# Normalising the transposed attention output from SBUF, and moving the dV products, in a one-core backward kernel

## The chip, the core and the metric

The kernel runs on one core of a Trainium2 chip. A core has a matrix engine (TensorE, PE in the profile), a vector engine (VectorE, DVE), an activation engine (ScalarE, ACT), a general engine (GpSimd, POOL) and a queue engine (SyncE, SP), each of which works through its own list of instructions in order and waits on semaphores for the others. Matrix products land in PSUM, which here is cut into eight banks of 128 partitions x 512 fp32; everything else lies in SBUF or in device memory. PEld in the profile is the loading of a matrix product's stationary operand.

The metric is the device time of one execution in microseconds (us). Before the change, three executions took 1052.82, 1053.05 and 1053.12 us, median 1053.05.

## What is computed

Two attention blocks over 2048 tokens of width 448 with 16 heads of 28, side by side, and the gradients of all their inputs and weights for a given `grad_out`. Block A is a linear attention; it fills the first 200 us and the change does not touch it. Block B is a multi-query attention, one key and one value head shared by 16 query heads:

```
scores = einsum("bhqd,bkd->bhqk", q, k) * (Dh ** -0.5)
p = _softmax(scores, axis=-1)
o = einsum("bhqk,bkd->bhqd", p, v)
out = o (heads side by side) @ wo
```

and `jax.vjp` of it: with dO the gradient of o, the kernel needs dV = P^T dO, dP = dO V^T, dS = P * (dP - D) with D the row sum of dO * o, dQ = dS K and dK = dS^T Q. The change lies in block B's main loop.

## The kernel before, in words

**Blocks and units.** The loop `for u in range(NU + 28)` (L926) runs over NU = 512 units. Eight units make a block b (64 blocks): a block is two heads (a pair) and 256 queries; a unit is 256 of the 2048 keys, in two halves of 128. "Unit 2 of a block" below is u = 8b + 2, and so on. Scores are kept transposed, keys on partitions. The work of one block is spread over several blocks' time: in the pass u the loop does the scores and exponentials of unit u, and the dP and dS of unit w = u - 16.

**One pass.** PE, in `rows_SD` (L683), writes the scores of two heads into two banks `sp` (S0, S1) of a ring of three, `SB`, and dP of unit w into the two banks `DB` (D0, D1); each bank takes two matmuls, one for each half of the keys, and uses 32 of the PE's rows: S0 and S1 lie on one half of the rows, D0 and D1 on the other. `todo` is the order of the eight matmuls. ACT then does exp of S0 (L946), a copy of D1 to SBUF, `cp` (L960), and exp of S1 (L992). DVE multiplies D0 by the exponentials of unit w (L958), POOL multiplies `cp` by those of the other head (L961); both write `dsT`. DVE transposes, in 32x32 blocks, the `dsT` of two passes earlier (L1039, `dsx`). There is only one D0 and one D1 bank: PE can write D0 of the next pass only after L958 has read this one, and D1 after L960.

**What PE does behind the rows.** Odd units: `dk_m`, sixteen matmuls for dK. Even units: `o_dq`, sixteen matmuls for o and dQ of two earlier units; the o sums of a block end in unit 0 of the next one. Behind `o_dq`, three of the four even units add dV: `dv_mm` multiplies one quarter (one head and 128 queries: four matmuls over 512 columns) of a block's dO/l, `don`, with the transposed exponentials `eN`. Two quarters come in unit 4, one in unit 6, one in unit 2 (L1006-1008).

**Once a block.** These steps borrow the third bank of `SB` for one pass, `spare` (L932). It was the S1 bank of the pass before, so it is free when that pass's L992 has read it, and it becomes the S0 bank of the next pass, whose first matmul therefore waits until the borrower has been read:

- unit 0: one part of the output projection (`out_proj`, sixteen small matmuls; in the early blocks `do_proj`), read by DVE at L747 (L913);
- unit 1: DVE copies o out of its bank to `oTs` (L974);
- unit 2: PE transposes `oTs` into the spare bank (`onat_T`, L809), and `o_norm` (L813) divides: DVE takes the reciprocal of the sums l out of the bank (L818, four elements a partition) and multiplies the bank by it into `oTs` (L819, 128 elements). POOL then forms `prod` = dO * o (L823), `don` = dO / l (L826), and copies o (L827);
- unit 3: DVE moves dQ out of its bank (L977); unit 4: DVE sums `prod` (L831), POOL scales the sum into `don` (L832);
- unit 6: PE transposes `don` into the spare bank (`don_T`, L840), DVE copies it (L847).

POOL further issues the store of a finished output tile once in four blocks (L749) and copies pieces of q (L851), up to two a block, in half of the blocks.

**What sets the order.** `tc.manual_schedule()`: each engine's instructions stand in the order in which the loop issues them, with no planner. So on DVE a pass is L958, then the once-a-block steps, then L1039. On PE a pass is the rows, then the once-a-block transposes or projection, then `dk_m` or `o_dq` with dV.

Of the kernel before, what the change touches and what calls it, by code (L numbers as in the profile page):

```python
# [9 lines left out]
ALU = mybir.AluOpType  # L10
# [7 lines left out]
P = 128  # L18
# [7 lines left out]
def kernel(  # L26
# [21 lines left out]
    nc = tc.nc  # L48
# [598 lines left out]
    NB = 64  # L647
# [3 lines left out]
    with ExitStack() as cs_:  # L651
# [20 lines left out]
        def eN(b, c):  # L672
            return ENs[(2 * b + c // 2) % 6][:, 16 * (c % 2):16 * (c % 2) + 16, :]

        def mmt(out, lhsT, rhs, pos, start, stop):
            nc.tensor.matmul(out, lhsT=lhsT, rhs=rhs, start=start, stop=stop, tile_position=pos,  # L676
                             skip_group_check=True)

        def blk(b):
            qc, pair = divmod(b, 8)  # L680
            return qc, pair, pair // 2, pair % 2

        def rows_SD(u, sp, dp):  # L683
            b, tp = divmod(u, 8)
            w = u - 16
            qc, pair, g, hp = blk(b)
            todo = [(0, 0), (0, 1), (1, 0), (1, 1)] * 2
            if sp is not None and dp is not None and u % 2 == 0:
                todo = [(0, 0), (0, 1), (1, 0)] * 2 + [(1, 1)] * 2
            seen = {}  # L690
            for d in todo:
                if (dp if d[0] else sp) is None:
                    continue
                k, h = d
                t2 = seen.get(d, 0)
                seen[d] = 1
                t = 2 * tp + t2
                tc_ = slice(t * P, (t + 1) * P)
                oc = slice(t2 * 256, (t2 + 1) * 256)
                r = 64 * (1 - hp if k else hp) + 32 * h  # L700
                if k:
                    mmt(dp[h][:, oc], vT_rep[r:r + 32, tc_], doT[w // 8][r:r + 32, :], (r, 0), True, True)
                else:
                    mmt(sp[h][:, oc], kT_rep[r:r + 32, tc_], qT_B[g][r:r + 32, qc * 256:(qc + 1) * 256],
                        (r, 0), True, True)
# [96 lines left out]
        def due(u, lag):  # L802
            b, r = divmod(u - lag, 8)
            return b if r == 0 and 0 <= b < NB else None

        def onat_T(b, bank):
            onp = bank[:, 0:P].rearrange("p (q h c) -> p q h c", q=2, h=2)
            for qb in range(2):
                nc.tensor.transpose(onp[:, qb, :, :].rearrange("p h c -> p (h c)"), oTs[0:64, qb * P:(qb + 1) * P],  # L809
                                    identF[0:64, 0:64], tile_position=(0, 0))  # L810
            onps[b] = onp

        def o_norm(b):  # L813
            onp = onps.pop(b)
            qc, pair, g, hp = blk(b)
            r_ = pw_.tile([P, 2, 2, 1], F32, name="rl")
            os_ = oTs[:, 0:P].rearrange("p (q h c) -> p q h c", q=2, h=2)
            nc.vector.reciprocal(out=r_[:], in_=onp[:, :, :, 0:1])  # L818
            nc.vector.tensor_tensor(out=os_, in0=onp[:, :, :, :], in1=r_[:].to_broadcast([P, 2, 2, 32]), op=ALU.mult)  # L819
            rl[b] = r_  # L820
            dnv = do_nat[:, 2 * qc:2 * qc + 2, pair * 64:pair * 64 + 64].rearrange("p q (h c) -> p q h c", c=32)
            prod[b] = pw_.tile([P, 2, 2, 32], F32, name="prod", bufs=1)
            nc.gpsimd.tensor_tensor(out=prod[b][:], in0=dnv, in1=os_, op=ALU.mult)  # L823
            dn = pw_.tile([P, 2, 2, 32], BF16, name="don", bufs=3)
            don[b] = dn
            nc.gpsimd.tensor_tensor(out=dn[:], in0=dnv, in1=r_[:].to_broadcast([P, 2, 2, 32]), op=ALU.mult)  # L826
            nc.gpsimd.tensor_copy(out=dnv, in_=os_)  # L827
# [32 lines left out]
        def dk_m(b, m, other=0):  # L860
            qc, pair, g, hp = blk(b)
            h, B, s = m // 8, (m // 2) % 4, m % 2
            for a in range(4):
                rhs = dsx[b][32 * a:32 * a + 32, :, h, :, :].rearrange(
                    "p u t (b i s) -> p u t b i s", b=4, s=2)[:, :, :, B, :, s]
                k = 32 * ((a + 2) % 4) if other else 32 * a
                mmt((dk_two if other else dk_acc)[k:k + 32, :],
                    qX[qc][32 * a:32 * a + 32, B, s, pair * 64 + 32 * h:pair * 64 + 32 * h + 32],
                    rhs, (32 * a, k), other == 2 or b == 0 and m == 0, other == 0 and b == NB - 1 and m == 15)
# [19 lines left out]
        def o_dq(vs, ys):  # L889
            for v, y in zip(vs, ys):  # L890
                todo = [f(i) for f, i in ((o_mm, v), (dq_mm, y)) if 0 <= i < NU]
                for _ in range(2):
                    for g_ in todo:
                        next(g_)

        def dv_mm(dv_acc, b, h, qb):
            for c in range(4):
                rhs = eN(b, c).rearrange("p (u h t q) k -> p u h t q k", u=2, h=2,
                                                       t=2)[:, :, h, :, qb, :]
                mmt(dv_acc[32 * c:32 * c + 32, :], don[b][:, qb, h, :], rhs, (0, 32 * c),  # L900
                    b == 0 and h + qb == 0, b == NB - 1 and h + qb == 2)
# [15 lines left out]
        with tc.manual_schedule():  # L917
# [8 lines left out]
            for u in range(NU + 28):  # L926
# [3 lines left out]
                sp = [SB[(2 * u + h) % 3] for h in range(2)] if hasS else None  # L930
                dp = DB if hasD else None
                spare = SB[(2 * u + 2) % 3] if hasS else DB[u // 4 % 2] if u > 530 else SB[2]  # L932
                rows_SD(u, sp, dp)
                if (b := due(u, 10)) is not None:
                    onat_T(b, spare)
                if (b := due(u, 14)) is not None:
# [10 lines left out]
                if u == 1:  # L947
                    q_shift(pn3, shifts[3], [pd_.tile([P, 2, 512], BF16, name="dsT").rearrange("p a b -> p (a b)").bitcast(F32)
                                             for _ in range(1)])
                    dv_acc = psA.tile([P, 512], F32, name="aacc")  # L950
# [24 lines left out]
                if (b := due(u, 27)) is not None:  # L975
                    qc, pair, g, hp = blk(b)
                    nc.vector.tensor_scalar(out=qT_B[g][64 * hp:64 * hp + 64, qc * 256:(qc + 1) * 256],  # L977
                                            in0=oq[64:128, 0:256], scalar1=scale, scalar2=None, op0=ALU.mult)
                if (b := due(u, 10)) is not None:
                    o_norm(b)  # L980
                    if b in (15, 31, 47, 55, 63):
                        t0, t1 = 2 * (b // 8) - 2 * (b < 48), 2 * (b // 8) + 2
                        nc.sync.dma_start_transpose(oTq[:, 4 * (t0 % 4):4 * (t0 % 4) + 4 * (t1 - t0), :],
                                                    do_nat[:, t0:t1, :].rearrange("p q c -> p (q c)"))
# [14 lines left out]
                if u % 2:  # L999
                    b, i = divmod(u - 27, 8)  # L1000
                    if 0 <= b < NB:
                        for m in range(2 * i, 2 * i + 4):
                            dk_m(b, m, (1 + (u == 519 and m == 2 * i + 1)) * (m % 2) if 519 <= u < 537 else 0)
                else:
                    o_dq((u - 2, u - 1), (u - 20, u - 19))
                    b, n = divmod(u - 20, 8)  # L1006
                    for k in {0: (0, 1), 2: (2,), 6: (3,)}.get(n, ()) if 0 <= b < NB else ():
                        dv_mm(dv_acc, b, k // 2, k % 2)
                y = u - 18

                if 512 <= u < 528 and u % 2 == 0:
# [23 lines left out]
                if 0 <= y < NU:  # L1035
                    b, tp = divmod(y, 8)
                    if tp == 0:
                        dsx[b] = px_.tile([P, 8, 2, 2, 256], BF16, name="dsx")
                    nc.vector.transpose(  # L1039
                        out=dsx[b][:, tp, :, :, :].rearrange("p h t c -> p (h t c)").bitcast(F32),  # L1040
                        in_=dsT[y][:, :, :].rearrange("p h c -> p (h c)").bitcast(F32))
# [14 lines left out]
        for c in range(4):  # L1056
# [3 lines left out]
                                           in1=dk_sum[32 * c:32 * c + 32, :].rearrange("p (t i) -> p t i", i=32),  # L1060
# [91 lines left out]
```

## Time and profile before

| | |
|---|---|
| three executions | 1052.82, 1053.05, 1053.12 us |
| profiled execution | 1052.68 us, span on the core 1050.9 us, granted clock 1.00 |
| busy over the span | PE 96%, DVE 85%, ACT 83%, POOL 76% |
| block A and block B's projections | up to about 207 us; first exp of the loop at 207.7 us |
| two blocks in the middle | 495.20 to 507.23 us (12.03 us) and 507.23 to 519.20 us (11.97 us) |
| DVE in those two | busy 11.82 and 11.77 us |
| ACT in those two | busy 11.96 and 11.90 us |
| POOL in those two | busy 10.37 and 10.85 us |

Busy times on the page are unions of spans, and spans of neighbours on one engine overlap by some 80 ns where they follow each other at once: a span holds the end of the pipeline, in which the next instruction already starts. So what an instruction takes from its engine is the distance from its start to the start of the next one, called its step here, and an engine that is never idle is recognised by steps that are always the same. Once the loop is full, its blocks take alternately 12.03 and 11.97 us, with few exceptions: odd blocks and even blocks differ by the half of the partitions on which their heads lie.

### The profile page before, as it was taken

How to read it: one execution, taken by the hardware profiler on the slowest of the kernel's cores; microseconds unless marked ns; L12 is line 12 of the kernel's file. 1: busy time of each engine (PE TensorE's matmuls, PEld its weight loads, DVE VectorE, ACT ScalarE, POOL GpSimd, SP SyncE). 2: the span in 40 equal slices, each digit the busy share in tenths (PEclk: the TensorE clock that was granted, in tenths of full speed). 3: DMA queues.
4: the chain of work that ended last, by engine and by line, in shares of the span. 5: the costliest groups of instructions: out<-in, count | busy, mean ns of one | idle time of the engine just before them, and what ended most of it. 6: DMA issues, size and time to landing. Idle time of an engine off the chain costs nothing.

```text
span 1050.9 us, 40033 instructions
## 1 busy us (share of the span) xinstructions
PE 1008.4 (96%) x16236; PEld 486.6 (46%) x16245; DVE 895.9 (85%) x1781; ACT 871.5 (83%) x1743; POOL 798.2 (76%) x1044
## 2 busy tenths in 40 slices
PE   9999999998999999999999999999999999999998
PEld 5555554434444444444444444444444444444444
DVE  6897500669999999999999999999999999999942
ACT  6463122589999999999999999999999999999632
POOL 8601272238888998899899989988998999888860
PEclk9999999999999999999999999999999999999999
DMA  9879999299999999999999999999999999999973
GB/s 266 150 134 192 189 222 215 42 163 202 188 196 190 188 195 198 194 193 191 197 175 195 192 202 185 204 199 184 192 194 191 194 190 193 204 186 182 220 156 87
DMA packets 689058, 195.15 MB, mean 186 GB/s; under 512 B 670408, under 2 KB 686688, under 8 KB 688872
## 3 DMA queue, kind: packets, MB, share of 16 engines
q1 hardware_dynamic: 680392, 179.97, 102.1%
q0 software_dynamic: 4544, 9.46, 3.4%
q10 hardware_dynamic: 3936, 3.16, 1.0%
q8 instruction: 127, 2.08, 0.8%
q14 instruction: 59, 0.48, 0.1%
HBM read 12.60 MB, written 10.84 MB: 22 GB/s over the span
## 4 chain that ended last, share of the span: by engine, by line
PE 44%; ACT 33%; issue 14%; DVE 6%; POOL 2%; DMA 0%; ACTq 0%; DVEq 0%; POOLq 0%
ACT cp L960 17%; ACT eT L992 13%; PE agen L81 13%; PE aacc L676 10%; PE agen L676 10%; PE aacc L81 6%; ACT eT L946 2%; DVE dsT L958 2%; PE aacc L809 2%; DVE dsx L1039 2%; PE aacc L840 1%; POOL dsT L961 1%; DMA out_dram<-dsT 0%; PE agen L313 0%; PE agen L227 0%
## 5 line engine op out<-in xcount | busy, mean ns | idle before, releaser
L961 POOL TENSOR_TENSOR dsT<-cp,eT 128x512 bf16<-128x512 bf16 x512 | 587.7, 1156 | 78.9 <-ACT cp L960 73.2
L1039 DVE STREAM_TRANSPOSE dsx<-dsT 128x512 f32<-128x512 f32 x512 | 357.8, 699 | 2.8 <-POOL dsT L961 0.7
L676 PEld LDWEIGHTS <-R 32*128 32x128 bf16 (+1 forms) x9104 | 228.5, 94 | 275.0 <-issue 239.4
L958 DVE TENSOR_TENSOR dsT<-agen,eT 128x512 bf16<-128x512 f32 x512 | 341.9, 668 | 10.6 <-PE agen L676 5.4
L960 ACT ACTIVATE cp<-agen 128x512 bf16<-128x512 f32 x512 | 315.8, 617 | 11.5 <-PE agen L676 10.5
L946 ACT ACTIVATE eT<-aacc 128x512 bf16<-128x512 f32 x512 | 313.6, 612 | 13.6 <-PE aacc L676 4.3
L992 ACT ACTIVATE eT<-aacc 128x512 bf16<-128x512 f32 x512 | 322.2, 629 | 0.0
L676 PE MATMUL agen<-dsx,qX 32*32 32x512 bf16 x4024 | 264.0, 376 | 0.0
L676 PE MATMUL agen<-doT,R 32*128 32x256 bf16 x2048 | 246.7, 269 | 4.2 <-DVE dsT L958 2.5
L676 PE MATMUL aacc<-R,R 32*128 32x256 bf16 (+1 forms) x2240 | 218.5, 269 | 7.1 <-DVE oTs L819 2.0
L676 PE MATMUL agen<-eT,R 128*32 128x256 bf16 x2048 | 157.4, 274 | 0.1
L676 PE MATMUL agen<-dsT,R 128*32 128x256 bf16 x2048 | 156.6, 274 | 0.1
L676 PEld LDWEIGHTS <-qX 32*32 32x32 bf16 x4096 | 78.2, 89 | 111.7 <-issue 53.3
L676 PE MATMUL aacc<-eN,don 128*32 128x512 bf16 x1024 | 96.7, 379 | 0.0
L81 PEld LDWEIGHTS <-R 128*128 128x128 bf16 x517 | 40.9, 98 | 42.2 <-issue 12.0
L81 PE MATMUL agen<-R,R 128*128 128x448 bf16 (+1 forms) x174 | 41.1, 360 | 1.8 <-ACT R L229 0.8
L851 POOL COPY qst<-R 128x512 bf16<-128x512 bf16 x56 | 34.2, 611 | 2.9 <-DMA qX<-qst 2.8
L823 POOL TENSOR_TENSOR prod<-R,oTs 128x128 f32<-128x128 bf16 x64 | 27.6, 431 | 9.3 <-DVE oTs L819 9.3
L676 PEld LDWEIGHTS <-don 128*32 128x32 bf16 x1024 | 33.8, 97 | 0.5
L586 DVE TENSOR_TENSOR osb<-R 32x512 bf16<-32x512 bf16 x4 | 1.7, 413 | 34.7 <-ACT R L583 34.7
L262 POOL TENSOR_SCALAR wdq<-wdq 128x448 bf16<-128x448 bf16 x16 | 21.1, 1327 | 12.9 <-DVE phiT L243 12.9
L427 POOL COPY pk<-R 128x256 bf16<-128x256 bf16 x4 | 1.6, 399 | 37.7 <-DVE R L389 37.7
(234 smaller groups left out, 983.1 us busy)
## 6 DMA issues: line engine op xcount, KB each, us to landing
eN<-eT SPq DMA_TRANSPOSE x128
xa<-in_A_x_dram SPq DMA_DIRECT2D x8, 224.0 KB
ga<-in_grad_out_dram SPq DMA_DIRECT2D x4, 448.0 KB
out_dram<-osb ACTq DMA_DIRECT2D x16, 112.0 KB
xa<-in_grad_out_dram POOLq DMA_DIRECT2D x4, 448.0 KB, 9.4
out_dram<-wdq POOLq DMA_DIRECT2D x8, 224.0 KB, 5.8
eT<-in_grad_out_dram SPq DMA_DIRECT2D x4, 448.0 KB
eT<-in_B_x_dram SPq DMA_DIRECT2D x4, 448.0 KB
```

The lines of the kernel that those rows point to most:

```text
L81: nc.tensor.matmul(out_ap, lhsT=lhsT, rhs=rhs, start=start, stop=stop, tile_position=(0, 0))
L262: nc.gpsimd.tensor_scalar(out=wq_n[:, st, 0:D], in0=wq_n[:, st, 0:D], scalar1=1.0, scalar2=None, op0=ALU.min)
L676: nc.tensor.matmul(out, lhsT=lhsT, rhs=rhs, start=start, stop=stop, tile_position=pos, skip_group_check=True)
L809: nc.tensor.transpose(onp[:, qb, :, :].rearrange("p h c -> p (h c)"), oTs[0:64, qb * P:(qb + 1) * P], identF[0:64, 0:64], tile_position=(0 ...
L823: nc.gpsimd.tensor_tensor(out=prod[b][:], in0=dnv, in1=os_, op=ALU.mult)
L851: eng.tensor_copy(out=st.rearrange("p (b s) a j -> p b s a j", s=2)[:, :, s, :, :], in_=src.unsqueeze(2).to_broadcast([P, 4, 4, 32]))
L946: nc.scalar.activation(out=eT(u)[:, 0, :], in_=sp[0][:, :], func=ACT.Exp, scale=scale)
L958: nc.vector.tensor_tensor(out=dst[:, 0, :], in0=dp[0][:, :], in1=ew[:, 0, :], op=ALU.mult)
L960: nc.scalar.activation(out=cp[:, :], in_=dp[1][:, :], func=ACT.Copy)
L961: nc.gpsimd.tensor_tensor(out=dst[:, 1, :], in0=cp[:, :], in1=ew[:, 1, :], op=ALU.mult)
L992: nc.scalar.activation(out=eT(u)[:, 1, :], in_=sp[1][:, :], func=ACT.Exp, scale=scale)
L1039: nc.vector.transpose(out=dsx[b][:, tp, :, :, :].rearrange("p h t c -> p (h t c)").bitcast(F32), in_=dsT[y][:, :, :].rearrange("p h c -> p ...
```

## The change

Three edits in the loop.

1. In `o_norm`, DVE first copies the transposed block (o and the sums l) out of the spare bank into `oTs`, then takes the reciprocal of the sums from `oTs`, then multiplies `oTs` by it in place. Before, the reciprocal and the product read the bank.
2. In `rows_SD`, odd units with both scores and dP take the order S0 S1 S0 S1 D0 D1 D0 D1 instead of S0 S1 D0 D1 S0 S1 D0 D1. Even units keep S0 S1 D0 S0 S1 D0 D1 D1 (the condition that kept the passes at either end of the loop out of this order is dropped).
3. The quarters of dV are issued right behind the rows instead of behind `o_dq`, and the quarter of unit 2 moves to unit 0 of the next block: two in unit 4, one in unit 6, one in unit 0.

```diff
-            todo = [(0, 0), (0, 1), (1, 0), (1, 1)] * 2
-            if sp is not None and dp is not None and u % 2 == 0:
+            todo = [(0, 0), (0, 1)] * 2 + [(1, 0), (1, 1)] * 2
+            if u % 2 == 0:
                 todo = [(0, 0), (0, 1), (1, 0)] * 2 + [(1, 1)] * 2
...
-            nc.vector.reciprocal(out=r_[:], in_=onp[:, :, :, 0:1])
-            nc.vector.tensor_tensor(out=os_, in0=onp[:, :, :, :], in1=r_[:].to_broadcast([P, 2, 2, 32]), op=ALU.mult)
+            nc.vector.tensor_copy(out=os_, in_=onp[:, :, :, :])
+            nc.vector.reciprocal(out=r_[:], in_=os_[:, :, :, 0:1])
+            nc.vector.tensor_tensor(out=os_, in0=os_, in1=r_[:].to_broadcast([P, 2, 2, 32]), op=ALU.mult)
...
                 rows_SD(u, sp, dp)
+                if u % 2 == 0:
+                    b, n = divmod(u - 20, 8)
+                    for k in {0: (0, 1), 2: (2,), 4: (3,)}.get(n, ()) if 0 <= b < NB else ():
+                        dv_mm(dv_acc, b, k // 2, k % 2)
...
                     o_dq((u - 2, u - 1), (u - 20, u - 19))
-                    b, n = divmod(u - 20, 8)
-                    for k in {0: (0, 1), 2: (2,), 6: (3,)}.get(n, ()) if 0 <= b < NB else ():
-                        dv_mm(dv_acc, b, k // 2, k % 2)
```

## The prediction, made before the changed kernel ran

> **What bounds the kernel now.** I read the page first, then busy times over two blocks of the loop, then DVE's timeline in them. On the page PE is the busiest engine and the loop looks full on four engines alike:
>
> ```profile
> PE 1008.4 (96%) x16236; PEld 486.6 (46%) x16245; DVE 895.9 (85%) x1781; ACT 871.5 (83%) x1743; POOL 798.2 (76%) x1044
> DVE  6897500669999999999999999999999999999942
> ACT  6463122589999999999999999999999999999632
> ```
>
> That does not say which one sets the pace, so I went to single steps. DVE's timeline over one odd block, 507.21 to 519.2:
>
> ```profile
> 507.92 0.28 DVE L747 CAST ot<-aacc 128x112 bf16<-128x112 f32 x1
> 508.11 0.70 DVE L1039 STREAM_TRANSPOSE dsx<-dsT 128x512 f32<-128x512 f32 x1
> 508.77 0.69 DVE L958 TENSOR_TENSOR dsT<-agen,eT 128x512 bf16<-128x512 f32 x1
> 509.38 0.41 DVE L974 COPY oTs<-agen 64x256 f32<-64x256 f32 x1
> ...
> 510.33 0.64 DVE L958 TENSOR_TENSOR dsT<-agen,eT 128x512 bf16<-128x512 f32 x1
> 510.91 0.16 DVE L818 RECIPROCAL rl<-aacc 128x4 f32<-128x4 f32 x1
> 511.10 0.29 DVE L819 TENSOR_TENSOR oTs<-aacc,rl 128x128 f32<-128x128 f32 x1
> 511.31 0.70 DVE L1039 STREAM_TRANSPOSE dsx<-dsT 128x512 f32<-128x512 f32 x1
> 511.93 0.66 DVE L958 TENSOR_TENSOR dsT<-agen,eT 128x512 bf16<-128x512 f32 x1
> 512.62 0.43 DVE L977 TENSOR_SCALAR R<-agen 64x256 bf16<-64x256 f32 x1
> ...
> 514.50 0.70 DVE L1039 STREAM_TRANSPOSE dsx<-dsT 128x512 f32<-128x512 f32 x1
> 515.12 0.65 DVE L958 TENSOR_TENSOR dsT<-agen,eT 128x512 bf16<-128x512 f32 x1
> 515.70 0.69 DVE L1039 STREAM_TRANSPOSE dsx<-dsT 128x512 f32<-128x512 f32 x1
> ```
>
> A transposition and the product behind it take 0.62 + 0.58 = 1.20 us from start to start where nothing holds them (514.50 to 515.70), and nearly the whole block is such steps. Where a pair takes longer, it waits for PE's D0: 0.07 us more in unit 1 (508.11 to 509.38, 1.27 us). The even block before it has the same 0.07 in unit 1, 0.07 in unit 7 (505.17 to 506.44) and 0.28 at its end (506.44 to 507.92). Around L977 and L847 steps are 0.11 longer each time, block after block; I count these as DVE's own. So DVE waits 0.07 + 0.42 = 0.49 us in 24.00 us of two blocks, and its own work is 23.51, or 11.76 us a block of 12.00. ACT's shortest step is 0.48 us, three a unit, 24 x 0.477 = 11.45 us a block: it has more to spare, and waits 0.25 us in unit 2 (L992 at 511.12, the next L946 at 511.85, 0.73 apart) and some 0.06 to 0.13 us behind the other even units. DVE bounds the loop, with 2% left.
>
> **The change, part by part.**
>
> *Copy before the division.* DVE now does L818 and L819 in 0.19 + 0.21 = 0.40 us. The new copy moves what L819 moves, from PSUM, so I take L819's 0.29; the reciprocal needs its result, and the row of L818 shows what that costs: 0.16 long, yet 0.19 to the next start, so 0.03 of gap. Copy 0.32. The reciprocal reads SBUF instead of PSUM; L831 (128 elements from SBUF) has a mean of 276 ns against L819's 292, so 0.015 less, 0.175. The product also, 0.19. Together 0.69: 0.29 to 0.30 us more on DVE, every block. Low end 0.19 (copy at L819's bare step 0.21, no gap), high end 0.33 (nothing gained from SBUF). The bank comes free when the copy ends, 0.29 after its start instead of 0.48: 0.19 earlier for the next scores. That cures most of ACT's 0.25, which pays only an engine that isn't the bound; 0 here.
>
> *What the product meets.* L819 has one operand in PSUM; the new product has both, `oTs` and `rl`, in SBUF. No DVE instruction of the loop is like that, and POOL is then at work:
>
> ```profile
> 510.15 2.38 POOL L961 TENSOR_TENSOR dsT<-cp,eT 128x512 bf16<-128x512 bf16 x2
> 512.48 0.42 POOL L823 TENSOR_TENSOR prod<-R,oTs 128x128 f32<-128x128 bf16 x1
> ```
>
> The nearest rows are DVE instructions with all operands in SBUF beside a POOL copy, just ahead of the loop; first the groups by shape, then the timeline, POOL and DVE:
>
> ```profile
> L627 DVE TENSOR_SCALAR gaT<-gaT 16x512 int32<-16x512 int32 x3 | 1.2, 415 | 3.8 <-ACT gaT L625 3.8
> L627 DVE TENSOR_SCALAR dsT<-dsT 16x512 int32<-16x512 int32 x1 | 0.8, 821 | 0.0
> ```
>
> ```profile
> 209.76 1.55 POOL L851 COPY dsT<-R 128x512 bf16<-128x512 bf16 x2
> 210.77 0.82 DVE L627 TENSOR_SCALAR dsT<-dsT 16x512 int32<-16x512 int32 x1
> ```
>
> The POOL copy ends at 211.31; L627 ends 0.28 later at 211.59 and takes 821 ns, where the three without POOL beside them take 415. The four DVE copies of L851 ahead of it end 0.28 after a POOL instruction's end too (two take 826 and 828 ns). On the other side stand L1039, whose 699 ns don't change beside POOL, but it has one input, and the L243 that lie inside POOL's L262 (1.33 us): 267 to 302 ns each, all but one (628). So a DVE instruction can be held to the end of a POOL instruction; whether this one is, the trace doesn't show. The new product starts at 510.91 + 0.32 + 0.18 = 511.41. POOL's second L961 starts when unit 2's `cp` is there, about 511.28, and ends at 512.53. Held that long, the product streams in its last 0.15 and ends near 512.67 instead of 511.69: 0.98 us, less some 0.03 because the scores of unit 1, and so `cp`, come a little earlier in the new order. I take 0.95; the low end is 0 (not held), the high end 1.15 (a whole L961). It is queued ahead of L1039 and of L958 of unit 3, so D0 stays unread, PE's rows of unit 4 stop at D0, and behind them ACT. POOL's L823 waits for the product too, 0.2 us, which POOL's 1.2 us of idle time in a block cover.
>
> The Trainium skill speaks against this edit (SBUF — State Buffer, "Who interferes with whom"): a DVE instruction with two SBUF inputs contends with a POOL instruction that reads SBUF, and the one that starts second is blocked until the first has finished. By that rule the sum is that with the hold; without it, that of the first rival. The trace agrees for L627 and L851 and has no instruction of this very kind.
>
> *Scores first in odd units.* PE starts the second pair of an order 0.11 to 0.12 us after the first (511.44 and 511.55). The second half of D0 becomes part of a third pair, at 0.22 instead of some 0.17: where DVE waits for D0 it waits 0.05 more, which is unit 1. In unit 5 the old order held S0's second half behind D0 (ACT's gap of 0.65 behind unit 4); that goes, on ACT, worth 0.
>
> *dV.* Four matmuls of a quarter take 0.21 us of PE. In unit 6 PE waits some 0.18 us for the spare bank, which ACT's L992 of unit 5 still reads; dV now fills that, and PE is 0.2 earlier in unit 7. In unit 0 the same wait stands before the output projection, so the added quarter costs 0.03. This takes DVE's waits in unit 7 and at the block's end (0.35 in two blocks) away, as does DVE's own delay. Were there no such wait in unit 0, the quarter would delay L747 by 0.2 us. `eN` is freed one even unit earlier; SP's queue gets no new instruction, and nothing on POOL or ACT moves.
>
> *Sum, a block:* DVE's work 11.76 + 0.30, the wait in unit 1 0.07 + 0.05: 12.18 without the hold, 0.18 over 12.00. With it, 13.13, 1.13 over. POOL's products run from u = 16 on, and with the slower blocks at the start I count 62 of them: 62 x 1.13 = 70 us. The profiled execution took 1052.7 us (span 1050.9, 1.8 around it), 0.4 under the median of the runs: 1053 + 70 = **1123 us**.
>
> **The rivals.**
>
> 1. *The product isn't held* (L243 speaks for it, L627 against), or starts just ahead of L961: its lead is only about 0.1 us. Then 62 x 0.18 = 11 us, **1064 us**; between 62 x 0.06 (no wait left in unit 1: 1057) and 62 x 0.36 (the waits of unit 7 and the block's end kept: 1075). A hold for part of L961 lies between, near 1090.
> 2. *Faster:* DVE is not full, because its three instructions run closer than the rows say. The point from which it decides is 0.12 us: 11.76 + 0.12 (unit 1) + 0.12 = 12.00. Then ACT's gaps count. At an addition of 0 it would be 62 x 0.12 = 7 us, **1046 us**. Against it: the copy alone has L819's 0.21.
> 3. *No change:* dV's gains and the new steps cancel, 1053; the addition would have to be 0.10 to 0.15.
>
> **How the numbers follow.** Held: 0.50 (1111 to 1136, 0.76 to 1.15 of hold); not held or hardly: 0.37; partly: 0.05; faster: 0.06; same within 0.2%, about what a measurement of this kernel can tell: 0.02. The likeliest is 1123. The range 1056 to 1136 leaves out the faster and unchanged cases and the tails, about 0.15. Slower: 0.50 + 0.37 + 0.05 = 0.92.
>
> **What would show it.** A block takes 13.1 us (held) or 12.2. The product on `oTs`, `rl` takes 1.2 us where L819 took 0.29, and ends just behind the L961 beside it; if it takes 0.28, the first rival is right. Copy and reciprocal take 0.29 and 0.15. PE's transposes of `don` follow dV without a wait; L958 in units 7 and 0 starts 0.6 behind L1039. Wrong altogether I would be if DVE showed idle time in each unit: then the bound lay elsewhere.

## The result and the profile after

The changed kernel takes 1131.22 us (median of four runs, 1128.79 to 1133.37) against 1052.99 us before: 1.074 times the time, 95% interval 1.0717 to 1.0768. The profiled execution took 1133.37 us, its span 1131.6 us, at a mean granted clock of 0.992.

The page of the changed kernel, busy lines and three groups of instructions (line, engine, operation, operands, count, then busy time, mean ns of one, idle time before and what ended it). L820 is the product that was L819, L963 the product on D0 that was L958, L824 the `prod` that was L823:

```profile
PE 1024.0 (90%) x16245; PEld 481.2 (43%) x16245; DVE 971.9 (86%) x1845; ACT 882.0 (78%) x1743; POOL 805.5 (71%) x1044
L676 PE MATMUL agen<-doT,R 32*128 32x256 bf16 x2048 | 232.6, 271 | 75.8 <-DVE dsT L963 72.3
L820 DVE TENSOR_TENSOR oTs<-oTs,rl 128x128 f32<-128x128 f32 x64 | 77.7, 1214 | 2.2
L824 POOL TENSOR_TENSOR prod<-R,oTs 128x128 f32<-128x128 bf16 x64 | 27.5, 430 | 23.8 <-DVE oTs L820 23.8
```

The same two groups in the kernel before:

```profile
L819 DVE TENSOR_TENSOR oTs<-aacc,rl 128x128 f32<-128x128 f32 x64 | 18.7, 292 | 2.3
L676 PE MATMUL agen<-doT,R 32*128 32x256 bf16 x2048 | 246.7, 269 | 4.2 <-DVE dsT L958 2.5
```

One product of 128 elements a partition takes 1214 ns where it took 292, 64 times: 59 us. PE's dP matmuls, which waited 4.2 us in all before, wait 75.8, nearly all of it for DVE's L963: that is D0, which DVE reads late.

The timelines of the same stretch, DVE and then POOL:

```profile
510.63 0.64 DVE L963 TENSOR_TENSOR dsT<-agen,eT 128x512 bf16<-128x512 f32 x1
511.21 0.27 DVE L818 COPY oTs<-aacc 128x128 f32<-128x128 f32 x1
511.51 0.18 DVE L819 RECIPROCAL rl<-oTs 128x4 f32<-128x4 f32 x1
511.72 1.26 DVE L820 TENSOR_TENSOR oTs<-oTs,rl 128x128 f32<-128x128 f32 x1
512.91 0.70 DVE L1041 STREAM_TRANSPOSE dsx<-dsT 128x512 f32<-128x512 f32 x1
```

```profile
511.68 1.16 POOL L966 TENSOR_TENSOR dsT<-cp,eT 128x512 bf16<-128x512 bf16 x1 [0.28 <-ACT cp L965]
513.07 0.43 POOL L824 TENSOR_TENSOR prod<-R,oTs 128x128 f32<-128x128 bf16 x1 [0.23 <-DVE oTs L820]
```

POOL's product starts 0.04 us before DVE's and ends at 512.84; DVE's ends 0.14 later, at 512.98. Over the whole loop the time that DVE's product takes follows from where it starts in POOL's: in the first block, with no POOL instruction beside it, it takes 0.29 us; where it starts 0.86 us behind POOL's (at 246.16) it takes 0.45, where it starts 0.31 behind (at 352.81) 0.99. Each of the held ones ends about 0.15 us behind POOL's product. A block now takes 13.23 or 13.25 us where it took 12.03 or 11.97. ACT and PE stand behind it: on ACT's timeline L997 starts at 512.91 and the next exp at 514.56.

```profile
514.56 0.60 ACT L951 ACTIVATE eT<-aacc 128x512 bf16<-128x512 f32 x1 [0.99 <-PE aacc L676]
```

### The profile page after: what moved, and what is told of

It reads as the page before. It is cut to its first block, busy times and chain, and to the rows that moved or that the text cites. A ratio compares the mean times of both kernels' runs of the same rounds, so it can differ in the third digit from the quotient of the medians.

```text
span 1131.6 us, 40114 instructions
## 1 busy us (share of the span) xinstructions
PE 1024.0 (90%) x16245; PEld 481.2 (43%) x16245; DVE 971.9 (86%) x1845; ACT 882.0 (78%) x1743; POOL 805.5 (71%) x1044
## 3 DMA queue, kind: packets, MB, share of 16 engines
q8 instruction: 127, 2.08, 0.7%
## 4 chain that ended last, share of the span: by engine, by line
DVE 42%; PE 42%; ACT 8%; issue 7%; DVEq 0%; DMA 0%; POOL 0%; ACTq 0%; POOLq 0%
DVE dsT L963 15%; PE agen L81 12%; DVE dsx L1041 12%; PE agen L676 11%; PE aacc L676 9%; DVE oTs L820 7%; PE aacc L81 5%; ACT cp L965 4%; ACT eT L997 3%; DVE R L982 2%; PE aacc L809 2%; DVE doT L848 2%; DVE oTs L818 1%; DVE rl L819 1%; DVE Dq L832 1%
## 5 line engine op out<-in xcount | busy, mean ns | idle before, releaser
L676 PEld LDWEIGHTS <-R 32*128 32x128 bf16 (+1 forms) x9104 | 245.8, 94 | 334.9 <-issue 290.0
L951 ACT ACTIVATE eT<-aacc 128x512 bf16<-128x512 f32 x512 | 316.3, 618 | 82.0 <-PE aacc L676 63.9
L1041 DVE STREAM_TRANSPOSE dsx<-dsT 128x512 f32<-128x512 f32 x512 | 357.5, 698 | 2.4 <-DVE R L747 0.2
L963 DVE TENSOR_TENSOR dsT<-agen,eT 128x512 bf16<-128x512 f32 x512 | 340.0, 664 | 14.2 <-PE agen L676 9.5
L965 ACT ACTIVATE cp<-agen 128x512 bf16<-128x512 f32 x512 | 315.3, 616 | 14.2 <-PE agen L676 12.6
L997 ACT ACTIVATE eT<-aacc 128x512 bf16<-128x512 f32 x512 | 320.6, 626 | 0.0
L676 PE MATMUL agen<-doT,R 32*128 32x256 bf16 x2048 | 232.6, 271 | 75.8 <-DVE dsT L963 72.3
L676 PE MATMUL agen<-dsx,qX 32*32 32x512 bf16 x4024 | 268.3, 380 | 0.0
L676 PE MATMUL aacc<-eN,don 128*32 128x512 bf16 x1024 | 91.7, 391 | 0.0
L820 DVE TENSOR_TENSOR oTs<-oTs,rl 128x128 f32<-128x128 f32 x64 | 77.7, 1214 | 2.2
L824 POOL TENSOR_TENSOR prod<-R,oTs 128x128 f32<-128x128 bf16 x64 | 27.5, 430 | 23.8 <-DVE oTs L820 23.8
L676 PEld LDWEIGHTS <-don 128*32 128x32 bf16 x1024 | 20.9, 94 | 41.7 <-issue 41.7
```

The source lines that it names most:

```text
L820: nc.vector.tensor_tensor(out=os_, in0=os_, in1=r_[:].to_broadcast([P, 2, 2, 32]), op=ALU.mult)
L951: nc.scalar.activation(out=eT(u)[:, 0, :], in_=sp[0][:, :], func=ACT.Exp, scale=scale)
L963: nc.vector.tensor_tensor(out=dst[:, 0, :], in0=dp[0][:, :], in1=ew[:, 0, :], op=ALU.mult)
L965: nc.scalar.activation(out=cp[:, :], in_=dp[1][:, :], func=ACT.Copy)
L997: nc.scalar.activation(out=eT(u)[:, 1, :], in_=sp[1][:, :], func=ACT.Exp, scale=scale)
L1041: nc.vector.transpose(out=dsx[b][:, tp, :, :, :].rearrange("p h t c -> p (h t c)").bitcast(F32), in_=dsT[y][:, :, :].rearrange("p h c -> p ...
```

## The experiments

The theory: the product is held because both its operands lie in SBUF while POOL runs a product that reads SBUF; the rest of the loss is DVE's longer work. The rivals: the product, written in place, is slow by itself; the copy and what follows it cost; the new orders cost.

**1. POOL moved out of the way.** The DVE instructions are those of the changed kernel.

```diff
-                    nc.gpsimd.tensor_tensor(out=dst[:, 1, :], in0=cp[:, :], in1=ew[:, 1, :], op=ALU.mult)
+                    if due(u, 10) is None:
+                        nc.gpsimd.tensor_tensor(out=dst[:, 1, :], in0=cp[:, :], in1=ew[:, 1, :], op=ALU.mult)
...
                     o_norm(b)
+                    if hasD:
+                        nc.gpsimd.tensor_tensor(out=dst[:, 1, :], in0=cp[:, :], in1=ew[:, 1, :], op=ALU.mult)
```

> The changed kernel with POOL's product of unit 2 (the dsT product of cp) placed behind POOL's three steps of the normalisation. POOL has then nothing to run while DVE's product of oTs and rl runs; the DVE instructions and their operands are those of the changed kernel. Hold theory (the product waits for the end of the POOL product beside it): the product takes about 0.28 us instead of 1.26, blocks of about 12.2 us, 1060 to 1070 us in all. Rival (the product is slow by itself: both operands in SBUF, written in place): still 1.2 us, 1131 us. Third possibility (POOL becomes late, since its product of unit 2 starts 1.4 us later and waits are carried on): product 0.28 us but blocks over 12.5 us.

1070.37 us, 1.0161 times before (1.0140 to 1.0182); blocks of 12.25 and 12.28 us. DVE's timeline, then POOL's:

```profile
504.76 0.27 DVE L818 COPY oTs<-aacc 128x128 f32<-128x128 f32 x1
505.06 0.18 DVE L819 RECIPROCAL rl<-oTs 128x4 f32<-128x4 f32 x1
505.27 0.29 DVE L820 TENSOR_TENSOR oTs<-oTs,rl 128x128 f32<-128x128 f32 x1
505.48 0.70 DVE L1044 STREAM_TRANSPOSE dsx<-dsT 128x512 f32<-128x512 f32 x1
```

```profile
503.77 1.15 POOL L967 TENSOR_TENSOR dsT<-cp,eT 128x512 bf16<-128x512 bf16 x1 [0.32 <-ACT cp L965]
505.64 0.43 POOL L824 TENSOR_TENSOR prod<-R,oTs 128x128 f32<-128x128 bf16 x1 [0.72 <-DVE oTs L820]
```

The same instruction, with POOL idle beside it, takes 0.29 us. In five of the 64 blocks POOL's product of the unit before still runs beside it, and there it takes 0.45 to 1.16 us and again ends some 0.15 us behind POOL's. It is not slow by itself: the neighbour on POOL was the cause.

**2. One operand back in PSUM.** POOL runs as in the changed kernel.

```diff
-            nc.vector.tensor_tensor(out=os_, in0=os_, in1=r_[:].to_broadcast([P, 2, 2, 32]), op=ALU.mult)
+            nc.vector.tensor_tensor(out=os_, in0=onp[:, :, :, :], in1=r_[:].to_broadcast([P, 2, 2, 32]), op=ALU.mult)
```

> The changed kernel, but the product reads o from the PSUM bank again; the copy to oTs and the reciprocal from oTs stay, so the bank is held through all three. Hold theory: only one operand in SBUF, so the product takes 0.29 us with POOL's product running beside it, and DVE has about 0.3 us a block more to do than before: blocks of 12.2 to 12.3 us, 1062 to 1075 us. Rival (the copy with the two steps behind it is what costs): product still long or blocks near 13 us.

1069.97 us, 1.0154 times before (1.0137 to 1.0171). DVE's and POOL's timelines:

```profile
504.91 0.18 DVE L819 RECIPROCAL rl<-oTs 128x4 f32<-128x4 f32 x1
505.13 0.29 DVE L820 TENSOR_TENSOR oTs<-aacc,rl 128x128 f32<-128x128 f32 x1
505.33 0.70 DVE L1041 STREAM_TRANSPOSE dsx<-dsT 128x512 f32<-128x512 f32 x1
```

```profile
505.09 1.16 POOL L966 TENSOR_TENSOR dsT<-cp,eT 128x512 bf16<-128x512 bf16 x1 [0.32 <-ACT cp L965]
```

POOL's product again starts 0.04 us ahead and runs on, and DVE's takes 0.29. So the hold needs POOL's product beside it, and it is gone when the product reads `o` from PSUM. The edit also ends the writing in place, so these runs don't show which of the two lifts it. The DVE copies of L851 ahead of the loop, which ended 0.28 us behind a POOL instruction, do not write in place, but they read only one operand. Both runs lie at 1070 us: the hold costs the rest, 61 us (some 6 us of slow clock, described in the last section, among them), and DVE's longer normalisation 17.

**3 and 4. The edits apart.** First the kernel before with the normalisation alone changed (edit 1 of the diff), then the changed kernel with the normalisation of before (edits 2 and 3).

```diff
-            nc.vector.reciprocal(out=r_[:], in_=onp[:, :, :, 0:1])
-            nc.vector.tensor_tensor(out=os_, in0=onp[:, :, :, :], in1=r_[:].to_broadcast([P, 2, 2, 32]), op=ALU.mult)
+            nc.vector.tensor_copy(out=os_, in_=onp[:, :, :, :])
+            nc.vector.reciprocal(out=r_[:], in_=os_[:, :, :, 0:1])
+            nc.vector.tensor_tensor(out=os_, in0=os_, in1=r_[:].to_broadcast([P, 2, 2, 32]), op=ALU.mult)
```

> The kernel before with the first edit alone (copy, reciprocal from oTs, product in SBUF). Hold theory: the product is held as in the changed kernel, 1125 to 1138 us. If the new order of scores or dV were what costs, near 1053 to 1065 us.

> The changed kernel with the normalisation as before, so the second and third edit alone (scores first in odd units, dV behind the rows and out of unit 2). If DVE's own work bounds the loop, only DVE's waits for D0 can go: those of unit 7 and of the block's end were 0.35 us in two blocks, unit 1 gets 0.05 more: 1042 to 1053 us. If ACT's gaps behind the even units set the pace, 0.3 us a block go: about 1034 us. If the new orders cost: over 1055 us.

The normalisation alone: 1130.88 us, 1.0730 times before (1.0711 to 1.0749), the whole of the change's loss. The orders alone: 1053.02 us, 0.9994 (0.9983 to 1.0005): no difference. ACT's gaps behind the even units don't set the pace: in an even block of the run with the orders alone the one behind unit 4 is gone (0.48 us from L996 to the next exp, the shortest there is, where the even block before had 0.65), and a new one stands behind unit 5 (0.62). Blocks take 11.93 and 11.97 us, hardly less than 12.03 and 11.97, and the whole run no less. The orders moved ACT's waiting about; DVE's own list didn't get shorter.

**5 to 7. The product off DVE.** If DVE bounds the loop, taking the product away from it must help. POOL can take it in one of its three steps; the diff is against the run with the orders alone:

```diff
-            nc.vector.reciprocal(out=r_[:], in_=onp[:, :, :, 0:1])
-            nc.vector.tensor_tensor(out=os_, in0=onp[:, :, :, :], in1=r_[:].to_broadcast([P, 2, 2, 32]), op=ALU.mult)
+            nc.scalar.activation(out=os_, in_=onp[:, :, :, :], func=ACT.Copy)
+            nc.vector.reciprocal(out=r_[:], in_=onp[:, :, :, 0:1])
...
-            nc.gpsimd.tensor_tensor(out=prod[b][:], in0=dnv, in1=os_, op=ALU.mult)
...
             nc.gpsimd.tensor_tensor(out=dn[:], in0=dnv, in1=r_[:].to_broadcast([P, 2, 2, 32]), op=ALU.mult)
-            nc.gpsimd.tensor_copy(out=dnv, in_=os_)
+            nc.gpsimd.tensor_tensor(out=prod[b][:], in0=dn[:], in1=os_, op=ALU.mult)
+            nc.gpsimd.tensor_tensor(out=dnv, in0=os_, in1=r_[:].to_broadcast([P, 2, 2, 32]), op=ALU.mult)
```

The sixth run has the changed kernel's copy and reciprocal on DVE in place of the first two added lines; the seventh is the fifth with the orders of before.

> The new orders of scores and dV, and a normalisation that takes the product off DVE: ACT copies the spare bank to oTs (between its copy of D1 and its second exp, where it waits for the bank anyway), DVE only takes the reciprocal from the bank, POOL multiplies dO by the reciprocal, that by the raw o, and the raw o by the reciprocal. DVE loses L819's step of 0.21 us a block, POOL's last step grows from 0.25 to about 0.45, ACT gets some 0.2 us a block in a gap of 0.27. If DVE's work bounds the loop: blocks of 11.73 to 11.8 us against 11.94 to 11.97 with the orders alone, 1038 to 1045 us. Rival (ACT and PE are as full as DVE, ACT's copy only moves the bound): 1050 to 1056 us.

> The changed kernel with its copy and its reciprocal on DVE, but the product on POOL instead of DVE (POOL's three steps as in the run with ACT's copy). No DVE instruction of the loop then has two operands in SBUF. Hold theory: no hold; DVE does 0.30 + 0.21 us where it did 0.40, 0.11 us a block more than with the orders alone: blocks of 12.05 us, 1056 to 1063 us. Rival (the copy's place or the earlier release of the bank costs the time): over 1068 us.

> The normalisation with ACT's copy and POOL's products, in the kernel before: old order of scores, dV where it was. If DVE's work alone set the pace of the kernel before, 0.21 us a block go here too: 1039 to 1046 us. If the old orders leave PE's rows as late as DVE was (the scores of odd units behind D0, dV behind the block's products), less than half of it comes: 1047 to 1053 us.

With ACT's copy: 1067.11 us, 1.0134 (1.0117 to 1.0150), and 1068.39 us with the old orders, 1.0143 (1.0124 to 1.0162). Both expectations missed. With DVE's copy: 1051.40 us, 0.9983 (0.9971 to 0.9995), better than expected. DVE's timeline of the fifth run shows why it missed:

```profile
502.59 0.64 DVE L962 TENSOR_TENSOR dsT<-agen,eT 128x512 bf16<-128x512 f32 x1
503.77 0.18 DVE L819 RECIPROCAL rl<-aacc 128x4 f32<-128x4 f32 x1 [0.54 <-ACT oTs L818]
```

DVE, the engine that was to be spared, waited 0.54 us a block for ACT: the reciprocal, which is issued behind ACT's copy of the same bank, is released by that copy, though both only read the bank. In the sixth run DVE's reciprocal, with no product to wait for it, takes a step of 0.10 us instead of 0.21, so that copy and reciprocal together cost DVE 0.40 us, what reciprocal and product cost before.

**8 and 9. The reciprocal ahead of ACT's copy,** with the new and with the old orders:

```diff
-            nc.scalar.activation(out=os_, in_=onp[:, :, :, :], func=ACT.Copy)
             nc.vector.reciprocal(out=r_[:], in_=onp[:, :, :, 0:1])
+            nc.scalar.activation(out=os_, in_=onp[:, :, :, :], func=ACT.Copy)
```

> As the run with ACT's copy and the new orders, but DVE's reciprocal is issued ahead of ACT's copy of the same bank. In that run the reciprocal started 0.54 us late, when ACT's copy had ended. If it waited because it stands behind that copy in program order: it now starts at once, DVE does 0.10 to 0.19 us where it did 0.40, ACT's copy comes some 0.05 us later than it could, and blocks take 11.65 to 11.8 us: 1034 to 1045 us. Rival (ACT's own load, three instructions a pass and the copy, is the next bound at about the same height): 11.85 us and more, 1046 to 1053 us.

> The same normalisation in the kernel before, with the old order of scores and dV where it was. If the new orders were neutral only because DVE's own work hid them, they are worth something here: this run 5 to 12 us slower than the one with the new orders, 1042 to 1053 us. If they are worth nothing anywhere: within 3 us of it.

1054.54 us, 1.0009 (1.0000 to 1.0018), and 1055.32 us, 1.0017 (1.0008 to 1.0026): the wait is gone, 12.6 us with it, and yet nothing is gained on the kernel before, and the eighth run misses both times of its expectation. The two lie 0.8 us apart, so the new orders are worth nothing here either. DVE's timeline of the eighth run, then PE's:

```profile
499.14 0.16 DVE L818 RECIPROCAL rl<-aacc 128x4 f32<-128x4 f32 x1
499.23 0.66 DVE L1040 STREAM_TRANSPOSE dsx<-dsT 128x512 f32<-128x512 f32 x1
500.23 0.69 DVE L962 TENSOR_TENSOR dsT<-agen,eT 128x512 bf16<-128x512 f32 x1 [0.34 <-PE agen L676]
```

```profile
499.22 0.28 PE L676 MATMUL agen<-dsT,R 128*32 128x256 bf16 x2
499.76 0.28 PE L676 MATMUL aacc<-R,R 32*128 32x256 bf16 x2 [0.27 <-ACT oTs L819]
```

DVE does 0.31 us less in unit 2 and then waits 0.34 us for D0 of unit 3, because PE's rows wait until ACT has copied the spare bank. So two things stand at about the same height there: DVE's list and the release of the bank. What came next was not ACT's own load, which I had named as the rival, but the bank that ACT held.

**10 and 11. Early release and less DVE together.** The sixth run, with DVE's reciprocal (and POOL's three steps behind it) issued after DVE's transposition of the same pass, so that it doesn't stand right behind the copy it reads (the transposes of finished o that SP issues in five of the blocks move along); then the same with the stores of finished tiles issued by SP.

```diff
             nc.vector.tensor_copy(out=os_, in_=onp[:, :, :, :])
+
+        def o_norm2(b):
...
             nc.vector.reciprocal(out=r_[:], in_=os_[:, :, :, 0:1])
...
                     nc.vector.transpose(
...
+                if (b := due(u, 10)) is not None:
+                    o_norm2(b)
```

```diff
-                nc.gpsimd.dma_start(out0[i * P:(i + 1) * P, D:2 * D], ots[i])
+                nc.sync.dma_start(out0[i * P:(i + 1) * P, D:2 * D], ots[i])
```

> The run with the copy and the reciprocal on DVE and the product on POOL, with the reciprocal (and POOL's steps) issued behind DVE's transposition of the same pass instead of right behind the copy. The copy's step of 0.30 us holds 0.09 in which DVE waits for its own result before the reciprocal; with the transposition between them that should go. If DVE's work bounds the loop: 0.09 us a block, 62 x 0.09 = 6 us less than that run: 1044 to 1048 us. Rival (PE's rows, which come late for DVE at the ends of even blocks, take it back): 1049 to 1053 us.

> The same, with the stores of finished output tiles issued by SP instead of POOL. In the run with the product on POOL a few blocks of 12.4 to 13.6 us stood among those of 11.9; in the one I followed, POOL was late behind such a store (0.58 us) and a copy of q (0.61 us), and DVE waited 0.53 us for prod. If POOL's lateness makes those blocks: 3 to 7 us less than without this edit, 1039 to 1046 us. If SP's queue, which carries the transposes of the exponentials, is delayed by the stores, or the long blocks have another cause: the same or slower.

1047.47 us, 0.9943 times before (0.9929 to 0.9957): the fastest version of all. DVE's timeline:

```profile
496.81 0.64 DVE L965 TENSOR_TENSOR dsT<-agen,eT 128x512 bf16<-128x512 f32 x1
497.38 0.27 DVE L816 COPY oTs<-aacc 128x128 f32<-128x128 f32 x1
497.58 0.68 DVE L1039 STREAM_TRANSPOSE dsx<-dsT 128x512 f32<-128x512 f32 x1
498.19 0.13 DVE L822 RECIPROCAL rl<-oTs 128x4 f32<-128x4 f32 x1
498.25 0.65 DVE L965 TENSOR_TENSOR dsT<-agen,eT 128x512 bf16<-128x512 f32 x1
```

From copy to transposition 0.20 us, from reciprocal to the next product 0.06: 0.26 instead of 0.40. Blocks take 11.77 and 11.79 us, 0.14 less than in the sixth run (11.90 and 11.93): in the usual blocks the steps taken off DVE's list show in full, with the bank released early. Over 62 blocks that would be 9 us; the run gained 4 on the sixth, because the long blocks among the others got longer (up to 14.15 us against 13.59). With the stores on SP: 1050.17 us, 0.9971 (0.9959 to 0.9983), 2.7 us more than without that edit. The usual blocks are the same, 11.75 to 11.80 us, and the long ones between them (12.1 to 14.4 us, some ten of 64 in both) are still there, mostly in the same places: POOL's stores are not what makes them. What does stays open.

## Why the prediction was right

The forecast of 1123 us, with the held product as the likeliest case, was right in its mechanism, and the measured 1131 lies inside that case's own range. The range on record, 1056 to 1136, held both the case with the hold and the one without it, so what counts is that the held case came, to which I had given 0.50. Term by term:

- *The hold:* taken as 0.95 us. The product's step is 1.19 us in the changed kernel and 0.21 in experiment 1: 0.98. By blocks it is 13.24 - 12.28 (experiment 2) = 0.96. It ends 0.14 behind the POOL product beside it, much as the row of L627 ahead of the loop had shown for another instruction (0.28). Experiments 1 and 2 show that it takes POOL's product and both operands in SBUF (or the writing in place). The margin was thinner than I had worked out: POOL's product was to start 0.13 us ahead (511.28 against 511.41) and starts 0.00 to 0.08 ahead in the usual blocks. What happens when DVE starts first, no block shows.
- *The rule of the Trainium skill* (SBUF — State Buffer, "Who interferes with whom"), two SBUF inputs against a POOL instruction that reads SBUF, the second to start being blocked until the first is finished: the trace agrees, with POOL 0.04 us ahead and 1.26 us for the product; with one input in PSUM (experiment 2) it took 0.29 in the same place. The rows of L627 and L851, which the prediction called in agreement with it, have one SBUF input each: they show a hold, not this rule's condition. The first rival, 1064 us, is what the two runs without a hold came to, 1070.
- *DVE's longer work:* taken as 0.29 to 0.30 us. Copy 0.30, reciprocal 0.21, product 0.21 make 0.72 against 0.40: 0.32. The reciprocal was mis-sized: I made its step shorter for reading SBUF (0.175), and it is 0.21; its mean is 179 ns against 159 from PSUM. The copy, 0.30 against 0.32, was near.
- *The wait in unit 1:* forecast to grow from 0.07 to 0.12; on DVE's timeline L1041 at 508.46 to L979 at 509.68 is 1.22 us against 1.20 with no wait: 0.02. The step "0.05 more for D0" failed; the second half of D0 did not come later for DVE.
- *The waits of unit 7 and of the block's end* were to go. That of unit 7 did. At the end of even blocks a pair still takes 0.76 + 0.74 us against 1.20, 0.30 more; in some 0.15. That step failed. Per block the first failure takes 0.10 us off and the second adds some 0.15, so the two cancel in part; with the 0.02 of the steps above that leaves 0.07 of the 0.10 by which a block without the hold, 12.28 us, is longer than the 12.18 of the forecast.
- *The orders* were costed at nothing but DVE's waits; experiment 4 has them at nothing, 0.9994. That ACT's gaps pay nothing was right.
- *Blocks counted:* 62 x 1.13 = 70 us. Measured 1.24 a usual block, which would make 77. In the two profiled executions the blocks 0 to 62 together differ by 79 us: some 6 of it lie in five blocks that were longer still, for a reason that no term had (last section), and the other 73 are less than 77 because early blocks of the kernel before were long already (block 5 took 13.24 us there and 13.25 in the changed kernel).

## What to carry to other kernels

Before copying an operand out of PSUM to free a bank, look at what is left for the instruction behind it: here, with both inputs in SBUF and a POOL product already running, it lasted until POOL's had ended, 1.26 us where it took 0.29. Keep one input in PSUM or give the product to POOL. Where an engine's steps follow one another at the same distance block after block, look at its list first: new orders of work on other engines gained nothing here (1053.02 us). A shorter list gains only as far as the next limit: 0.31 us off it gained nothing in experiment 8, where the bank was released later, and 0.14 showed in full in the usual blocks of experiment 10. A result that is read by the very next instruction of its engine costs 0.1 us more here than one with another instruction between them, so put independent work there.

## What the runs showed of the hardware that was not expected

*PE at half clock in a full loop.* Five of the changed kernel's blocks take 14.5 to 14.8 us, and in each lies a stretch in which the granted clock was halved. The busy time of three stretches of the changed kernel (length, then busy time and count of PE, PEld, DVE, ACT and POOL, granted clock, DMA share, GB/s):

```profile
586.00:590.00 4.00, 3.99 (x97) 1.95 (x91) 3.79 (x8) 3.98 (x9) 3.58 (x5) 1.00 0.47 89
582.50:586.00 3.50, 3.50 (x46) 1.12 (x46) 2.50 (x4) 2.14 (x5) 1.90 (x3) 0.51 1.18 224
579.10:582.51 3.41, 2.18 (x44) 0.99 (x40) 3.31 (x8) 2.42 (x6) 2.78 (x5) 1.00 1.03 156
```

The first line is just behind the slow stretch, the second is the stretch itself: half as many matmuls in a like time. The third is the 3.41 us just ahead of it. Five such stretches of 3.41 us stand in the profiled execution (at 316.3, 582.5, 637.1, 691.7 and 1039.9 us); a block with one takes about 1.3 us more, so they make some 6 us. The kernel before had none but at its very end. Two stand in the run with the normalisation alone, one in that with the stores on SP, none in the others but at their very ends. The changed kernel's PE stands still for about 1 us once a block:

```profile
514.24 0.26 PE L676 MATMUL agen<-doT,R 32*128 32x256 bf16 x1 [1.02 <-DVE dsT L963]
```

Such a standstill lies in the 3.41 us ahead of each of the five stretches. There PE is busy for 2.18 us, 64%, where it is busy 88% of the time from 500 to 582.5 us (72.47 of 82.50). Ahead of the three stretches of the two other runs it is 2.06, 2.08 and 2.10 us. But other stretches of that length with as little (2.10 us from 244.59 on) brought no drop, so this is not the whole condition, and that the standstill makes the clock drop was not tried. The Trainium skill (TensorE: Matmul & The Clock Gate, "What's actually happening") has a gate that halves the clock after an idle window of some 3.4 us: the length and the half agree with 3.41 us and 0.51, but the window ahead of these stretches was not idle, with PE busy for 2.18 of its 3.41 us. The granted clock also goes with the spread of the four runs: 0.998 at 1128.8 us, 0.992 at 1133.4.

*The distance that a result costs.* The same copy takes a step of 0.30 us with the reciprocal of its result behind it and 0.20 with a transposition behind it; the reciprocal 0.21 with the product behind it, 0.10 or 0.06 without. The length of an instruction changes with it too: a reciprocal of four elements takes 179 ns right behind the copy whose result in SBUF it reads, and 129 from the same SBUF tile with a transposition between them (experiment 10); from PSUM it takes 159. So it isn't SBUF that made it longer.
